# Retention and mixture of experts on one core: a list read as it lies, gate operations a tile sooner, and four smaller edits

## Chip, cores and metric

The kernel runs as one program on one core of a Trainium2 chip. The metric is device time in microseconds (us), lower is better. TensorE does matrix products, VectorE, ScalarE and GpSimd (POOL in the profile) work element by element, and SyncE (SP) issues most of the DMAs.

## The reference

Retention over 8 sequences of 576 positions, 8 heads of 64, then a layer of 8 experts in which every token goes to the one with the highest logit:

```python
scores = q @ k.T / sqrt(64)                       # (8, 8, 576, 576)
D[h, i, j] = gamma[h] ** (i - j) if i >= j else 0 # gamma = 1 - 2 ** (-5 - h)
x = (scores * D) @ v                              # -> (4608, 512), heads side by side
logits = x @ w_gate                               # (4608, 8)
e_idx = argmax(logits);  gate_w = softmax(logits)[e_idx]
eom = sigmoid(x @ w_output_gate)
for e in range(8):                                # w1: 512 x 1024, w2: 1024 x 512
    y = relu(x[e_idx == e] @ w1[e]) @ w2[e]
    out[e_idx == e] = gate_w * eom[:, e] * y
```

## The kernel before

**Tiles.** The 4608 positions are 36 tiles of 128; tile g is `c = g % 9` within a run of 9 tiles, which is two sequences. The loop over g is the first half of the program, the experts are the second. Every engine executes its instructions in the order in which the code issues them (`manual_schedule`): the order is written by hand, and an instruction that waits holds up all that stand behind it on its engine.

**One tile.** A tile's q, k and v come as three thirds of one buffer `pk` (768 KB, five buffers), issued by SP: the first five tiles in `load_first`, later ones in two parts (q and k, then v) in `load`. GpSimd scales q and v by powers of gamma into `qs` (L351) and `vs` (L356). Those factors `gq_sb` are made by ScalarE at the start (`factors`, L126) from two inputs gq and gk. TensorE transposes k (`k_rows`, L363), makes the scores `sc` one tile ahead (L385) into three PSUM banks, multiplies state and scores into one buffer `o_ps` (`out_x`, L416 and L420) and adds to the state (L402). VectorE masks the scores into `S_sb` (L389). ScalarE copies `o_ps` to `xT`, and VectorE transposes it into the rows of x (`x_rows`, L437); after these two `o_ps` is free for the next tile. SP stores the rows to `xs` in DRAM.

The three banks are zeroed before the loop with products of a zero operand (L555).

**Gating.** Every four tiles make a group of 512 tokens, n = 0 to 8. TensorE makes its logits (L448) at the end of one tile's turn, then the work on them is spread over the next three turns: `gate_a` on VectorE (maxima, the one-hot `oh` and its sum, L451 to L476), `ranks` on TensorE (L486 to L493), `gate_b`, `gate_d` and `gate_c` on VectorE, which end in `meta`, a token's number and weight. GpSimd scatters each token's entry to its slot in its expert's list in DRAM (`lst`, L536), one DMA for 128 tokens.

**From lists to experts.** An expert's list is taken in two parts: part 0 is its first 360 entries, part 1 the next 256. For expert 0 part 0 holds only tokens of the first six groups, so that it can be read before the loop ends. `load_idx` (SP) loads lists of 16-word entries, spread over four quarters of the partitions, and `make_idx` (VectorE) turns them into `idx` (token and weight) and `gidx`, with one operation at L307 and four copies at L311:

```python
rest = NS[part] > 32 * nb
...
        if g == 31:
            make_idx(0, 2, 0)
        if g + 1 < NTILE:
            prep_v(g + 1)
        if 30 < g < 33:
            for t in (0, 1) if g == 31 else (2,):
                gather_rows(t)
```

GpSimd gathers x from `xs`: for expert 0 whole rows by `idx` (`gather_rows`, L199), into a `pk` buffer in part 0 and transposed by TensorE; for the others quarter rows by `gidx` (`gather`, L186), transposed by VectorE. Expert 0's three tiles of part 0 have 128, 128 and 104 rows.

**The experts.** Each product is made in fp32r as three of split halves (hi by hi, hi by lo, lo by hi). Weights are cast by `upper` (ScalarE, the hi half, L160) and `lower` (VectorE, the rest). `mm1` (L250) makes a block of hidden rows over 360 or 256 columns, `mm2` (L266) the output of one tile; ScalarE scales it (L271) and GpSimd scatters the rows to the output (L272). `some(n)` issues the next n waiting scatters or gathers on GpSimd.

Of the kernel before, what the change touches and what calls it, by code (L numbers as in the profile page):

```python
# [51 lines left out]
def tile_retention_moe(  # L52
# [137 lines left out]
    def gather_rows(t, dep=None):  # L190

        if t == 0:
            rows = ld.tile([P, 3, 512], F32, name="pk")
# [5 lines left out]
        after(G.indirect_dma_start(out=XG[0, t], out_offset=None, in_=xs[0:n, :],  # L199
                                   in_offset=bass.IndirectOffsetOnAxis(ap=idx[:, 0, t, 0:1], axis=0),  # L200
                                   bounds_check=n - 1, oob_is_err=False), dep)
# [73 lines left out]
    lists1 = []

    def load_idx(e0, e1, part):
        s0, t0, nb = part * NS[0], part * 4 * TA, NB[part]
# [4 lines left out]
        dmas = []
        if e1 - e0 < 4:

            for e in range(e0, e1):
                v = view[e, :, s0:s0 + 32 * nb].rearrange("a (j t) w -> a j (t w)", t=nb).broadcast_to([4, 32, LW * nb])
                dmas.append(SP.dma_start(out=lists[:, e, t0:t0 + nb].rearrange("p t w -> p (t w)"), in_=v))
                if rest:
                    v = view[e, :, s0 + 32 * nb:s0 + 32 * nb + 32].broadcast_to([4, 32, LW])  # L290
                    dmas.append(SP.dma_start(out=lists[:, e, t0 + nb], in_=v))
        for a in range(4):
            if e1 - e0 >= 4:
                v = view[e0:e1, 0, s0:s0 + 32 * nb].rearrange("e (j t) w -> j e (t w)", t=nb)
                dmas.append(SP.dma_start(out=lists[32 * a:32 * a + 32, e0:e1, t0:t0 + nb].rearrange("j e t w -> j e (t w)"),
                                         in_=v))
                if rest:
                    v = view[e0:e1, 0, s0 + 32 * nb:s0 + 32 * nb + 32].rearrange("e j w -> j e w")
                    dmas.append(SP.dma_start(out=lists[32 * a:32 * a + 32, e0:e1, t0 + nb], in_=v))
# [4 lines left out]
    def make_idx(e0, e1, part):
        n, t0 = (TA, 0) if part == 0 else (CT - TA, TA)
        lists = lists0 if (e0, part) == (0, 0) else lists1[0]
        V.tensor_scalar(out=gidx[:, e0:e1, 4 * t0:4 * (t0 + n)], in0=lists[:, e0:e1, 4 * t0:4 * (t0 + n), 0],  # L307
                        scalar1=4.0, scalar2=quad, op0=ALU.mult, op1=ALU.add)
        for a in range(4):
            q = slice(32 * a, 32 * a + 32)  # L310
            V.tensor_copy(idx[q, e0:e1, t0:t0 + n],  # L311
                          lists[q, e0:e1].rearrange("j e (t u) w -> j e t u w", u=4)[:, :, t0:t0 + n, a, 0:2])
# [138 lines left out]
    def gate_a(n):  # L451
# [10 lines left out]
        V.tensor_tensor(out=fst, in0=fst, in1=desc.broadcast_to([P, GT, E]), op=ALU.mult)
# [91 lines left out]
    for b in banks:  # L554
        T.matmul(b.rearrange("p a b -> p (a b)"), lhsT=zw[:, 0:P], rhs=zw, start=True, stop=True)  # L555
# [326 lines left out]
```

## Time and profile before

| | |
|---|---|
| time, median of 3 runs | 605.94 us (604.21 to 612.22) |
| profiled execution, its own time | 606.38 us |
| its span, first to last instruction | 604.6 us |
| mean granted TensorE clock | 0.994 of full |
| busy: TensorE (PE) | 576.1 us, 95% of the span |
| busy: VectorE (DVE), GpSimd (POOL), ScalarE (ACT) | 327.7, 315.6 and 169.7 us |
| scores of tile 1, 32, 33, 34 and 35 begin | at 10.04, 128.63, 131.76, 140.11 and 143.89 us of the span |

The profile is one execution. PE stands for TensorE's products, PEld for its loads of the stationary operand, which lie beside products; SPq is SP's issue of a DMA. In a row of the timeline stand the start in us of the span, the duration, the engine, the line of the code, the operation, what it writes and reads (`out<-in`), its shape and type, how many instructions stand in a row (x), and in brackets the idle time of the engine before it and what ended that. A row of the waits has the engine, what it was to write and on which line, the engine, buffer and line it waited for, the sum of the waits in us, their number and the longest of them. A row of a stretch has its bounds, its length, for each engine the busy time and the number of instructions, the granted clock, the share of the DMA engines and GB/s.

### The profile page before, as it was taken

To read this page: it belongs to the slowest core of one execution; us is meant where nothing else is said; L and a number is where in the kernel's file an instruction comes from. 1 tells how busy PE (TensorE), PEld (TensorE's weight loads), DVE (VectorE), ACT (ScalarE), POOL (GpSimd) and SP (SyncE) were. 2 spreads that over 40 slices of the span, in tenths; PEclk is the share of its full clock that TensorE was granted. 3 is DMA by queue.
4 is the path that set the end of the run, shared out by engine and by line. 5 is a ranking of instruction groups with operands and counts; after the bars stand their busy time and mean duration, and the time that the engine had idled before them with its cause. 6 is when DMAs were issued, how large, how long until landed. Compare 5 with 4: busy or idle time off the path is not lost. (4 is left out here: it accounts for less than half of the span.)

```text
span 604.6 us, 14060 instructions
## 1 busy us (share of the span) xinstructions
PE 576.1 (95%) x5737; PEld 507.2 (84%) x5737; DVE 327.7 (54%) x655; ACT 169.7 (28%) x360; POOL 315.6 (52%) x333
## 2 busy tenths in 40 slices
PE   7999999888798999999999999999999999999995
PEld 4888888777696889779978997998899799889974
DVE  3566777674661869736732961584186249426300
ACT  5434334333341222132212221222222222212210
POOL 4768898867276734363553455446344535540011
PEclk9999999998999999999999999999999999999998
DMA  8999899877646436323621642262155216321001
GB/s 304 297 321 287 275 277 292 250 212 237 175 116 214 123 127 225 93 89 114 200 98 58 192 149 75 81 232 96 48 179 165 82 53 218 118 68 52 1 36 44
DMA packets 53324, 94.78 MB, mean 157 GB/s; under 512 B 9018, under 2 KB 30971, under 8 KB 53258
## 3 DMA queue, kind: packets, MB, share of 16 engines
q1 hardware_dynamic: 43594, 73.03, 38.2%
q0 software_dynamic: 9232, 20.23, 10.3%
q8 instruction: 46, 0.75, 0.5%
q10 hardware_dynamic: 432, 0.59, 0.3%
q14 instruction: 20, 0.16, 0.1%
HBM read 74.33 MB, written 20.15 MB: 156 GB/s over the span
## 5 line engine op out<-in xcount | busy, mean ns | idle before, releaser
L186 POOL DMA_INDIRECT x_q<-xs,gidx x140 | 148.7, 1062 | 113.2 <-ACT hh L254 70.9
L250 PE MATMUL h_ps<-xh,w1h 128*128 128x360 f32 (+1 forms) x512 | 154.6, 302 | 2.6 <-issue 1.3
L250 PE MATMUL h_ps<-xl,w1h 128*128 128x360 f32 (+1 forms) x512 | 154.6, 302 | 0.3 <-issue 0.3
L250 PE MATMUL h_ps<-xh,w1l 128*128 128x360 f32 (+1 forms) x512 | 154.5, 302 | 0.0
L266 PE MATMUL y_ps<-w2h,hh 128*128 128x512 f32 (+1 forms) x320 | 125.2, 391 | 2.4 <-ACT y L271 1.4
L266 PE MATMUL y_ps<-w2h,hl 128*128 128x512 f32 (+1 forms) x320 | 124.9, 390 | 0.5 <-DVE hl L255 0.5
L266 PE MATMUL y_ps<-w2l,hh 128*128 128x512 f32 (+1 forms) x320 | 124.8, 390 | 0.0
L272 POOL DMA_INDIRECT out_dram<-y,idx x40 | 41.1, 1028 | 122.6 <-ACT y L271 111.9
L250 PEld LDWEIGHTS h_ps<-xh,w1h 128*128 128x128 f32 x512 | 96.1, 188 | 3.5 <-issue 1.8
L250 PEld LDWEIGHTS h_ps<-xh,w1l 128*128 128x128 f32 x512 | 97.1, 190 | 0.2 <-issue 0.2
L250 PEld LDWEIGHTS h_ps<-xl,w1h 128*128 128x128 f32 x512 | 96.1, 188 | 1.1 <-issue 0.5
L254 ACT ACTIVATE hh<-h_ps 128x360 fp32r<-128x360 f32 (+1 forms) x128 | 54.5, 429 | 149.5 <-PE h_ps L250 126.6
L255 DVE SCALAR_TENSOR_TENSOR hl<-h_ps,hh 128x360 fp32r<-128x360 f32 (+1 forms) x128 | 58.6, 474 | 69.0 <-ACT hh L254 58.2
L266 PEld LDWEIGHTS y_ps<-w2h,hh 128*128 128x128 f32 (+1 forms) x320 | 58.8, 184 | 16.6 <-ACT y L271 1.8
L266 PEld LDWEIGHTS y_ps<-w2h,hl 128*128 128x128 f32 (+1 forms) x320 | 58.8, 184 | 15.3 <-DVE hl L255 1.3
L266 PEld LDWEIGHTS y_ps<-w2l,hh 128*128 128x128 f32 (+1 forms) x320 | 58.8, 184 | 13.4
L271 ACT ACTIVATE y<-y_ps,idx 128x512 f32<-128x512 f32 (+1 forms) x40 | 27.5, 689 | 129.7 <-issue 75.3
L389 DVE TENSOR_TENSOR S_sb<-sc,cmat_sb 128x512 f32<-128x512 f32 x72 | 46.1, 681 | 32.2 <-PE sc L385 29.6
L223 DVE TENSOR_TENSOR xl<-x_t,xh 128x512 fp32r<-128x512 f32 (+1 forms) x35 | 23.5, 672 | 63.9 <-ACT xh L220 61.9
L351 POOL TENSOR_TENSOR qs<-pk,gq_sb 128x512 f32<-128x512 f32 x36 | 46.2, 1282 | 13.4 <-DMA pk<-in_pack_dram 6.6
L536 POOL DMA_INDIRECT lst<-meta,sli x36 | 36.1, 1004 | 27.1 <-DVE meta L532 15.6
L420 PE MATMUL o_ps<-S_sb,vs 128*64 128x128 f32 x576 | 40.4, 281 | 1.8 <-DVE xq L437 0.7
(126 smaller groups left out, 604.3 us busy)
## 6 DMA issues: line engine op xcount, KB each, us to landing
st<-in_w_dram SPq DMA_DIRECT2D x61, 512.0 KB
pk<-in_pack_dram SPq DMA_DIRECT2D x31, 512.0 KB
pk<-in_pack_dram SPq DMA_DIRECT2D x35, 256.0 KB
xs<-xq SPq DMA_DIRECT2D x40, 128.0 KB
pk<-in_pack_dram SPq DMA_DIRECT2D x3, 768.0 KB
x_q<-xs,gidx POOLq DMA_INDIRECT x140
xs<-w2h SPq DMA_DIRECT2D x16, 128.0 KB
xs<-w2l SPq DMA_DIRECT2D x16, 128.0 KB
```

The costliest lines, as they stand in the source:

```text
L186: after(G.indirect_dma_start(out=XG[e, t][:, u, :], out_offset=None, in_=xs.rearrange("t (a c) -> (t a) c", a=4), in_offset=bass.IndirectO ...
L223: V.tensor_tensor(out=lo, in0=src[:, :, 0:n], in1=hi.bitcast(F32), op=ALU.subtract)
L250: T.matmul(ps, lhsT=a[:, k, :], rhs=b[:, k, :], start=(j == 0), stop=(j == 3 * KB - 1))
L254: done = A.activation(out=hh, in_=ps, func=AF.Relu)
L255: V.scalar_tensor_tensor(out=hl, in0=ps, scalar=0.0, in1=hh.bitcast(F32), op0=ALU.max, op1=ALU.subtract)
L266: i = T.matmul(ps, lhsT=a[:, c0:c0 + n], rhs=b, start=(j == 0), stop=(j == 3 * FB - 1))
L271: A.activation(out=y, in_=ps, func=AF.Copy, scale=idx.bitcast(F32)[0:n, e, t, 1:2])
L272: G.indirect_dma_start(out=out, out_offset=bass.IndirectOffsetOnAxis(ap=idx[0:n, e, t, 0:1], axis=0), in_=y, in_offset=None, bounds_check= ...
L351: G.tensor_tensor(out=qs[g], in0=pk[g][:, 0].rearrange("p (n i) -> p n i", n=NP), in1=gq_sb[:, c % 5], op=ALU.mult)
L389: V.tensor_tensor(out=S_sb[:, r].rearrange("p (a b) i -> p a b i", a=2), in0=sc[r].rearrange("p (a b) i -> p a b i", a=2), in1=m, op=ALU.mult)
L420: last = T.matmul(part(p, r), lhsT=vs[g][:, 2 * p + r, :], rhs=S_sb[:, r, p, :], start=(state is None and p < 2), stop=True, skip_group_ch ...
L536: i = G.indirect_dma_start(out=lst, out_offset=bass.IndirectOffsetOnAxis(ap=sli[:, t, :], axis=0), in_=m[:, t, :], in_offset=None)
```

## The change

Six edits:

1. **Expert 0's list as it lies.** `load_rows` loads a part of expert 0's list by one DMA: in part 0, 120 partitions take three entries each, so a partition's entry t is a row of tile t. The gathers and the scaling of y use these entries (`entry`) directly. `make_idx` for expert 0 goes; expert 0's tiles of part 0 have 120 rows each (`N0`). The list of expert 1 is loaded at g = 32 in place of g = 29, its index step stands behind the loop, and those of the other lists stand together after the first transpose of expert 1. At g = 31 GpSimd gathers one tile in place of two, at g = 32 two in place of one.
2. **Gate operations a tile sooner.** `gate_a` is cut in two. Its first four operations (transpose, maximum, two comparisons) come right behind the logits, so ahead of the next masks; the others are `gate_e` at the old place.
3. **Parts.** Tile 2 is loaded in three parts and tiles 3 and 4 in two; the second half of `cmat` comes after tile 3.
4. **One bank in bfloat16.** The third bank is zeroed by a product of bfloat16 operands.
5. **A first copy.** A memset of `bump` on VectorE and a copy of it on ScalarE stand ahead of `factors`.
6. **Casts.** The first weight cast comes at the end of turn g = 33, and two behind the loop; before, they stood at g = 33, 34 and 35 ahead of the turn's `out_x`.

```diff
@@ gather_rows
             for i in range(TA):
-                XG[0, i] = rows[:, i]
+                XG[0, i] = rows[0:N0, i]
...
-                                   in_offset=bass.IndirectOffsetOnAxis(ap=idx[:, 0, t, 0:1], axis=0),
+                                   in_offset=bass.IndirectOffsetOnAxis(ap=entry(0, t)[:, 0:1], axis=0),
...
-    def where(t):
+    def where(e, t):
         part = 0 if t < TA else 1
-        t0 = t - part * TA
-        return part, P * t0, min(P, NS[part] - P * t0)
+        t0, w = t - part * TA, P if e or part else N0
+        return part, w * t0, min(w, NS[part] - w * t0)
+
+    def entry(e, t):
+        part, _, n = where(e, t)
+        return idx[0:n, e, t] if e else rows0[part][0:n, t - part * TA]
...
+    def load_rows(part):
+        n = where(0, part * TA)[2]
+        v = lst[part * NS[0]:part * NS[0] + NS[part], :].rearrange("(p t) w -> p (t w)", p=n)
+        read_after(SP.dma_start(out=rows0[part][0:n].rearrange("p t w -> p (t w)"), in_=v))
...
@@ load_first
-        for i in range(3):
-            SP.dma_start(out=pk[1][:, i], in_=pack[1, :, i])
-        SP.dma_start(out=pk[2], in_=pack[2])
-        SP.dma_start(out=cmat_sb[:, 1], in_=cmat[:, 1])
+        for g in range(1, 3):
+            for i in range(3):
+                SP.dma_start(out=pk[g][:, i], in_=pack[g, :, i])
         for g in range(3, 5):
-            SP.dma_start(out=pk[g], in_=pack[g])
+            for p in (slice(0, 2), slice(2, 3)):
+                SP.dma_start(out=pk[g][:, p], in_=pack[g, :, p])
+            if g == 3:
+                SP.dma_start(out=cmat_sb[:, 1], in_=cmat[:, 1])
@@ gate_a
         V.tensor_tensor(out=lm, in0=l, in1=bc(mx), op=ALU.subtract)
+        gt["fst"] = fst
+
+    def gate_e(n):
+        fst, lm = gt["fst"], gt["lm"]
...
@@ ahead of the loop
-    for b in banks:
-        T.matmul(b.rearrange("p a b -> p (a b)"), lhsT=zw[:, 0:P], rhs=zw, start=True, stop=True)
+    for i, b in enumerate(banks):
+        z = zw.bitcast(BF16)[:, 0:512] if i == 2 else zw
+        T.matmul(b.rearrange("p a b -> p (a b)"), lhsT=z[:, 0:P], rhs=z, start=True, stop=True)
+
+    V.memset(bump, 0.0)
+    A.activation(out=bump[:, 0:1], in_=bump[:, 1:2], func=AF.Copy)
@@ the loop
-        if g == 31:
-            make_idx(0, 2, 0)
...
-            for t in (0, 1) if g == 31 else (2,):
+            for t in (0,) if g == 31 else (1, 2):
                 gather_rows(t)
...
-        if 32 < g < 35:
-            low.append(upper(*wl.pop(0)))
         if n >= 0 and 0 < late < 3:
-            (gate_a, gate_b)[late - 1](n)
+            (gate_e, gate_b)[late - 1](n)
         if g == 35:
...
-            low.append(upper(*wl.pop(0)))
...
             logits(n, gt["ps"])
+            gate_a(n)
...
         if g == 29:
-            load_idx(0, 2, 0)
+            load_rows(0)
+        if g == 32:
+            load_idx(1, 2, 0)
+        if g == 33:
+            low.append(upper(*wl.pop(0)))
...
+    low += [upper(*wl.pop(0)) for _ in range(2)]
     lower(*low.pop(0))
...
@@ experts
-    load_idx(0, 2, 1)
+    make_idx(1, 2, 0)
+    load_rows(1)
+    load_idx(1, E, 1)
     load_idx(2, E, 0)
-    load_idx(2, E, 1)
...
-    make_idx(0, 2, 1)
     some(2)
...
     transp(1, 0)
+    make_idx(1, E, 1)
     make_idx(2, E, 0)
-    make_idx(2, E, 1)
```

**On VectorE, one tile of the loop with the gate operations, before** (`x_rows` is L437; `w2h` and `xq` are its buffers; the masks are L389, the gate L454 to L475):

```order
L437 STREAM_TRANSPOSE w2h_2310<-o_ps 128x4x4x32
L389 TENSOR_TENSOR S_sb<-sc_132,cmat_sb 128x512
L389 TENSOR_TENSOR S_sb<-sc_133,cmat_sb 128x512
L454 STREAM_TRANSPOSE lg_ps<-lg_ps 128x128
L458 TENSOR_REDUCE mx<-lg_ps 128x4
L459 TENSOR_TENSOR lg_ps<-lg_ps,mx 128x32
L461 TENSOR_TENSOR lm<-lg_ps,mx 128x32
L462 TENSOR_TENSOR lg_ps<-lg_ps,csm_sb 128x32
L464 TENSOR_REDUCE m_2381<-lg_ps 128x4
L470 TENSOR_TENSOR oh<-lg_ps,m_2381 128x32
L475 TENSOR_REDUCE oh<-oh 128x8
L437 STREAM_TRANSPOSE w2h_2310<-o_ps 128x4x4x32
```

The same place with the change, where `x_rows` is L449, the masks are L401 and the gate is L466 to L492:

```order
L449 STREAM_TRANSPOSE w2h_2318<-o_ps 128x4x4x32
L466 STREAM_TRANSPOSE lg_ps<-lg_ps 128x128
L470 TENSOR_REDUCE mx<-lg_ps 128x4
L471 TENSOR_TENSOR lg_ps<-lg_ps,mx 128x32
L473 TENSOR_TENSOR lm<-lg_ps,mx 128x32
L401 TENSOR_TENSOR S_sb<-sc_138,cmat_sb 128x512
L401 TENSOR_TENSOR S_sb<-sc_139,cmat_sb 128x512
L479 TENSOR_TENSOR lg_ps<-lg_ps,csm_sb 128x32
L481 TENSOR_REDUCE m_2389<-lg_ps 128x4
L487 TENSOR_TENSOR oh<-lg_ps,m_2389 128x32
L492 TENSOR_REDUCE oh<-oh 128x8
L449 STREAM_TRANSPOSE w2h_2318<-o_ps 128x4x4x32
```

Four operations have moved ahead of the two masks; four still stand between the masks and the transpose that frees `o_ps`.

**On VectorE, turn 31, before** (L531 and L532 end the group's `meta`, L307 and L311 are the index step):

```order
L531 RECIPROCAL meta_87<-lg_ps 128x4
L532 COPY meta_87<-toks 128x4
L307 TENSOR_SCALAR gidx<-lists_89,csm_sb 128x2x12
L311 COPY idx<-lists_89 32x2x6 x4
L437 STREAM_TRANSPOSE w2l_2484<-o_ps 128x4x4x32
L389 TENSOR_TENSOR S_sb<-sc_132,cmat_sb 128x512
L389 TENSOR_TENSOR S_sb<-sc_133,cmat_sb 128x512
```

With the change:

```order
L548 RECIPROCAL meta_87<-lg_ps 128x4
L549 COPY meta_87<-toks 128x4
L449 STREAM_TRANSPOSE w2l_2489<-o_ps 128x4x4x32
L401 TENSOR_TENSOR S_sb<-sc_138,cmat_sb 128x512
L401 TENSOR_TENSOR S_sb<-sc_139,cmat_sb 128x512
```

The five operations on the lists are gone from between `meta` and the transpose.

**On GpSimd, turns 31 and 32, before** (L199 is the gather of expert 0's rows; after `idx` it needs nothing of VectorE):

```order
L351 TENSOR_TENSOR qs<-pk,gq_sb 128x512
L356 TENSOR_TENSOR vs<-pk,gk_sb 128x512
L199 DMA pk<-xs,idx 128x512 x2
L351 TENSOR_TENSOR qs<-pk,gq_sb 128x512
L356 TENSOR_TENSOR vs<-pk,gk_sb 128x512
L199 DMA pk<-xs,idx 128x512
L351 TENSOR_TENSOR qs<-pk,gq_sb 128x512
L356 TENSOR_TENSOR vs<-pk,gk_sb 128x512
```

With the change:

```order
L363 TENSOR_TENSOR qs<-pk,gq_sb 128x512
L368 TENSOR_TENSOR vs<-pk,gk_sb 128x512
L201 DMA pk<-xs,rows_90 120x512
L363 TENSOR_TENSOR qs<-pk,gq_sb 128x512
L368 TENSOR_TENSOR vs<-pk,gk_sb 128x512
L201 DMA pk<-xs,rows_90 120x512 x2
L363 TENSOR_TENSOR qs<-pk,gq_sb 128x512
L368 TENSOR_TENSOR vs<-pk,gk_sb 128x512
```

The gathers stand in the same places, one and two in place of two and one; their offsets are now the rows that SP's DMA brings (`rows_90`), not VectorE's `idx`.

More of the change, by code (lines that the diff above doesn't have):

```diff
@@ L32 @@
 NW = (384, 256)
+N0 = 120
 CAP = sum(NS)
@@ L97, in tile_retention_moe @@
     meta = [const.tile([P, GT, LW], I32, name=f"meta{i}") for i in range(2)]
-    lists0 = const.tile([P, 2, TA * 4, LW], I32, name="lists0")
+    lists0 = const.tile([P, 1, TA * 4, LW], I32, name="lists0")
+    rows0 = [const.tile([P, n, LW], I32, name=f"rows{i}") for i, n in enumerate((TA, CT - TA))]
     idx = const.tile([P, E, CT, 2], I32, name="idx")
@@ L215, in split_x @@
     def split_x(e, t, src):
-        part, c0, n = where(t)
+        part, c0, n = where(e, t)
         hi, lo = (a[:, :, c0:c0 + n] for a in xt_of(e, part))
@@ L227, in transp_pe @@
     def transp_pe(t, src):
+        n = where(0, t)[2]
         for k in range(KB):
-            T.transpose(src[:, k, :], XG[0, t][:, P * k:P * k + P], ident)
+            T.transpose(src[:, k, 0:n], XG[0, t][:, P * k:P * k + P], ident[0:n, 0:n])
         return split_x(0, t, src)
@@ L258, in mm2 @@
     def mm2(e, t, between={}):
-        part, c0, n = where(t)
+        part, c0, n = where(e, t)
         ps = pools["ps_y"].tile([P, DM], F32, name="y_ps")[0:n]
@@ L280, in load_idx @@
         rest = NS[part] > 32 * nb
-        lists = lists0 if (e0, part) == (0, 0) else lists1[0]
+        early = (e0, part) == (1, 0)
         view = lst[0:E * NT, :].rearrange("(e a s) w -> e a s w", e=E, a=1)
[L283 to L299, printed above, removed]
@@ L300, in load_idx @@
-        for i in dmas:
-            for j in scat:
-                tc.add_manual_dep(i.ins, j.name, SYNC, reason="reads the list after every scatter so far")
+        if early:
+            v = view[1, :, s0:s0 + 32 * nb].rearrange("a (j t) w -> a j (t w)", t=nb).broadcast_to([4, 32, LW * nb])
+            read_after(SP.dma_start(out=lists0[:, 0, t0:t0 + nb].rearrange("p t w -> p (t w)"), in_=v))
+            v = view[1, :, s0 + 32 * nb:s0 + 32 * nb + 32].broadcast_to([4, 32, LW])
+            read_after(SP.dma_start(out=lists0[:, 0, t0 + nb], in_=v))
@@ new lines, in load_idx, with read_after @@
+        for a in () if early else range(4):
+            q = slice(32 * a, 32 * a + 32)
+            v = view[e0:e1, 0, s0:s0 + 32 * nb].rearrange("e (j t) w -> j e (t w)", t=nb)
+            read_after(SP.dma_start(out=lists1[0][q, e0:e1, t0:t0 + nb].rearrange("j e t w -> j e (t w)"), in_=v))
+            if rest:
+                v = view[e0:e1, 0, s0 + 32 * nb:s0 + 32 * nb + 32].rearrange("e j w -> j e w")
+                read_after(SP.dma_start(out=lists1[0][q, e0:e1, t0 + nb], in_=v))
+    def read_after(i):
+        for j in scat:
+            tc.add_manual_dep(i.ins, j.name, SYNC, reason="reads the list after every scatter so far")
@@ L304, in make_idx @@
     def make_idx(e0, e1, part):
         n, t0 = (TA, 0) if part == 0 else (CT - TA, TA)
-        lists = lists0 if (e0, part) == (0, 0) else lists1[0]
-        V.tensor_scalar(out=gidx[:, e0:e1, 4 * t0:4 * (t0 + n)], in0=lists[:, e0:e1, 4 * t0:4 * (t0 + n), 0],
+        lists = lists0 if (e0, part) == (1, 0) else lists1[0][:, e0:e1]
+        V.tensor_scalar(out=gidx[:, e0:e1, 4 * t0:4 * (t0 + n)], in0=lists[:, :, 4 * t0:4 * (t0 + n), 0],
                         scalar1=4.0, scalar2=quad, op0=ALU.mult, op1=ALU.add)
@@ L311, in make_idx @@
             V.tensor_copy(idx[q, e0:e1, t0:t0 + n],
[L312 removed]
+                          lists[q].rearrange("j e (t u) w -> j e t u w", u=4)[:, :, t0:t0 + n, a, 0:2])
     actx = ExitStack()
@@ L459, in gate_a @@
         V.tensor_tensor(out=fst, in0=l, in1=bc(mx), op=ALU.is_equal)
-        lm = sm.tile([P, GT, E], F32, name="lm")
+        lm = gt["lm"] = sm.tile([P, GT, E], F32, name="lm")
         V.tensor_tensor(out=lm, in0=l, in1=bc(mx), op=ALU.subtract)
+        gt["fst"] = fst
+    def gate_e(n):
+        fst, lm = gt["fst"], gt["lm"]
+        bc = lambda a: a.broadcast_to([P, GT, E])
         V.tensor_tensor(out=fst, in0=fst, in1=desc.broadcast_to([P, GT, E]), op=ALU.mult)
@@ L639, in tile_retention_moe @@
     gt["ps"] = ps_1.tile([P, 512], F32, name="lg_ps")
-    mm1(0, 0, 0, {5: lambda: (logits(NG - 1, gt["ps"]), gate_a(NG - 1))})
+    mm1(0, 0, 0, {5: lambda: (logits(NG - 1, gt["ps"]), gate_a(NG - 1), gate_e(NG - 1))})
     mm1(0, 0, 1, {9: lambda: ranks(NG - 1)})
```

4 lines of the change are left out of this document (2 added, 2 removed).

## Prediction

> **What bounds the kernel now.** I read the page's busy shares first, then TensorE's busy time stretch by stretch.
>
> ```profile
> PE 576.1 (95%) x5737; PEld 507.2 (84%) x5737; DVE 327.7 (54%) x655; ACT 169.7 (28%) x360; POOL 315.6 (52%) x333
> core 0: us, PE busy (x) PEld busy (x) DVE busy (x) ACT busy (x) POOL busy (x), PEclk, DMA share, GB/s
> 0.00:15.00 15.00, 11.04 (x160) 6.84 (x162) 4.73 (x11) 8.19 (x24) 6.48 (x10) 1.00 0.89 304
> 100.00:150.00 50.00, 44.67 (x1004) 37.44 (x996) 30.53 (x92) 17.02 (x38) 39.21 (x48) 0.97 0.78 245
> 150.00:200.00 50.00, 43.39 (x296) 37.63 (x297) 26.27 (x66) 16.70 (x31) 29.28 (x33) 1.00 0.55 159
> 300.00:400.00 100.00, 100.00 (x569) 89.48 (x568) 51.12 (x76) 23.81 (x47) 48.90 (x47) 1.00 0.36 117
> ```
>
> TensorE is busy 576.1 of 604.6 us. From 300 to 400 us it has no gap, and the change leaves the experts' products alone there. So only the other 28.5 us can be won, plus time in which TensorE runs at a lower clock, and the edits sit in three of the stretches that hold it: the start, the loop over tiles, and the loop's end at about 130 us. I take them in order, against the profiled execution's 606.38 us (span 604.6 and 1.8 around it); that is 0.44 above the median of the three runs, 605.94, so I carry no correction.
>
> **The start.** The chain to the third tile's scores (sc, L385), from the timeline:
>
> ```profile
> 1.46 5.28 PE L555 MATMUL sc<-xh 128*128 128x512 f32 x6 [1.46 <-DVE xh L552]
> 6.07 1.28 ACT L126 ACT_TABLE_LOAD   x1 [6.07 <-DMA gk_sb<-in_gk_dram]
> 7.37 1.28 ACT L126 ACTIVATE gq_sb<-gq_sb,gk_sb 128x128 f32<-128x128 f32 x4
> 8.72 1.26 POOL L351 TENSOR_TENSOR qs<-pk,gq_sb 128x512 f32<-128x512 f32 x1 [1.32 <-ACT gq_sb L126]
> 10.04 0.90 PE L385 MATMUL sc<-qs,pk 64*64 64x128 f32 x32 [1.89 <-POOL qs L351]
> 12.30 1.27 POOL L351 TENSOR_TENSOR qs<-pk,gq_sb 128x512 f32<-128x512 f32 x1 [2.31 <-DMA pk<-in_pack_dram]
> 13.62 0.90 PE L385 MATMUL sc<-qs,pk 64*64 64x128 f32 x32 [0.61 <-POOL qs L351]
> 10.00:15.00 5.00, 4.35 (x118) 3.81 (x120) 2.42 (x4) 4.27 (x16) 2.70 (x3) 1.00 1.01 384
> ```
>
> *Table load.* ScalarE stands on gk until 6.07, and only then loads its table. The added copy needs nothing but a memset, so the 1.28 us load lies in that wait, and the factors, qs of tile 1 and sc of tile 1 each come 1.28 us earlier: sc at about 8.8. *Tile 2 in parts.* qs of tile 2 needs the first third alone, but waits for the whole 768 KB. The two other thirds, 512 KB (0.524 MB), take 1.4 us at the 384 GB/s of the last row, so qs starts at about 10.9 and sc of tile 2 at 12.2 instead of 13.62: 1.4 us. Both links move by about the same, so neither becomes the new stop. Bounds for the pair: 0 if the parts land no sooner than the whole, 2.3 (all of POOL's wait) if they land at once; I take **1.4**, from the rate, between the two. Four more DMA issues on SP lie before SP's next work, which waits for sc of tile 1.
>
> *One bank zeroed in bfloat16.* Six passes take 5.28 us, so the third bank's two take 1.76. A bfloat16 product over 512 columns isn't in the trace; its price lies between 0 and those 1.76 us, and I put it at half of one pass, 0.44, so that zeroing ends near 5.4. This is off the chain above (qs of tile 1 decides) and counts 0. The two more instructions at the head (memset, copy) stand in idle time of their engines.
>
> [...] Here the same run of 5.28 us was followed by full speed; a shorter one isn't shown.
>
> **The loop over tiles.** Five cycles of four tiles, from scores to scores, in a table by stretch (the sum), and what TensorE waits for between 30 and 147 us:
>
> ```profile
> sum 75.88, PE 72.58 PEld 62.19 DVE 54.63 ACT 27.68 POOL 65.40; mean PE 14.52 PEld 12.44 DVE 10.93 ACT 5.54 POOL 13.08
> PE o_ps L416 <- DVE w2l L437: 2.2, 1, 2.2
> PE o_ps L416 <- DVE xq L437: 1.2, 2, 0.7
> PE o_ps L416 <- DVE w2h L437: 1.1, 2, 0.6
> PE o_ps L420 <- DVE xq L437: 0.7, 1, 0.7
> ```
>
> A cycle lasts 15.18 us, of which TensorE works 14.52. It waits for L437, VectorE's transpose that frees the only o_ps buffer. One such place, all of VectorE and TensorE that bears on it:
>
> ```profile
> 103.26 1.08 PE L448 MATMUL lg_ps<-xT,wg_sb 128*32 128x128 f32 x32
> 104.28 0.90 PE L385 MATMUL sc<-qs,pk 64*64 64x128 f32 x32
> 105.24 1.29 DVE L389 TENSOR_TENSOR S_sb<-sc,cmat_sb 128x512 f32<-128x512 f32 x2 [1.57 <-PE sc L385]
> 106.44 0.32 DVE L454 STREAM_TRANSPOSE lg_ps<-lg_ps 128x128 f32<-128x128 f32 x1
> 107.48 0.20 DVE L462 TENSOR_TENSOR lg_ps<-lg_ps,csm_sb 128x32 f32<-128x32 f32 x1
> 108.31 0.70 DVE L437 STREAM_TRANSPOSE xq<-o_ps 128x512 f32<-128x512 f32 x1
> 108.45 0.17 PE L493 MATMUL lg_ps<-oh,cbf_sb 128*128 128x8 bf16 x1
> 109.16 0.67 PE L416 MATMUL o_ps<-qs,stT 64*64 64x128 f32 x16 [0.55 <-DVE xq L437]
> ```
>
> The gate operations run from 106.44 to 108.31, ahead of L437. The change moves the first four (106.44 to 107.48, 1.04 us) ahead of S_sb, where VectorE idles 1.57 us. They need the logits, done at about 104.3, so they end at 105.35 and push S_sb from 105.24 to 105.35: 0.1 us, and S_sb is used a whole tile later (it is made before the previous tile's products), so that push is covered. Then come the other gate operations, 0.83, and L437 starts at about 107.5 instead of 108.31 and ends at 108.2, while TensorE finishes its ranks at 108.6: the gap of 0.55 goes. The rows by DVE w2h and xq sum to 3.0 over five places; two smaller ones stand under ACT's names. I take **3.2** for the stage. Bounds: 0 (something else holds the tile), and 0.66 a cycle over seven cycles, 4.6.
>
> **The end of the loop.** Here lies the list of expert 0. SP's issues, VectorE, POOL and TensorE in the timeline, and the same time in two stretches:
>
> ```profile
> 127.67 0.65 SPq L288 DMA_DIRECT2D lists<-lst  x1
> 128.26 1.04 POOL L356 TENSOR_TENSOR vs<-pk,gk_sb 128x512 f32<-128x512 f32 x1
> 129.56 0.54 SPq L291 DMA_DIRECT2D lists<-lst  x1
> 131.76 0.90 PE L385 MATMUL sc<-qs,pk 64*64 64x128 f32 x32
> 133.16 0.24 DVE L307 TENSOR_SCALAR gidx<-lists,csm_sb 128x24 int32<-128x24 int32 x1 [1.64 <-DMA lists<-lst]
> 133.31 0.69 DVE L311 COPY idx<-lists 32x12 int32<-32x12 int32 x4
> 134.04 0.72 DVE L437 STREAM_TRANSPOSE w2l<-o_ps 128x512 f32<-128x512 f32 x1
> 134.90 0.67 PE L416 MATMUL o_ps<-qs,stT 64*64 64x128 f32 x16 [2.24 <-DVE w2l L437]
> 134.91 1.07 POOL L199 DMA_INDIRECT pk<-xs,idx  x1 [5.61 <-DMA xs<-w2h]
> 137.32 1.28 POOL L351 TENSOR_TENSOR qs<-pk,gq_sb 128x512 f32<-128x512 f32 x1
> 132.70:135.00 2.30, 0.10 (x4) 0.13 (x8) 1.74 (x7) 0.00 (x0) 0.09 (x1) 1.00 1.07 328
> 136.10:139.50 3.40, 3.40 (x46) 2.90 (x46) 0.72 (x1) 1.43 (x4) 3.19 (x3) 0.50 1.06 395
> ```
>
> VectorE stands 1.64 us for the lists and makes idx until 134.0, with L437 queued behind it, and TensorE loses **2.24**. POOL's row names a DMA, but it too starts when idx is done. In the change nothing on VectorE waits: one DMA replaces four, its rows are the offsets themselves, and L437 can follow at 131.5, ahead of TensorE's need at 132.6. Right behind the gap the clock is 0.50 for 3.4 us in which TensorE is fully busy: half of it, **1.7**, is lost time. I credit both, 3.9.
>
> The wait moves to POOL, whose gather of the rows now stands for the new list with qs and vs queued behind it. Lists issued last at 129.56 to 130.1 served VectorE at 133.16, 3.1 us on; the new DMA goes out at 127.67 to 128.3, so it lands at about 131.4 at the latest. With one gather (1.07 and 0.3 of issue) qs of tile 34 ends near 134.1; TensorE asks for it a tile (14.52 / 4 = 3.6 us) after 131.76, at 135.4. So POOL's wait is covered by 1.3 us. The two other gathers stand a tile later, behind vs. SP issues 0.65 instead of 2.4 us there, and its later loads come sooner. Bounds: 0 if POOL's new wait stops TensorE for as long, 4.2 with the shorter issue.
>
> [...]
>
> **The rest.** Three weight casts on ScalarE come later, two of them behind the last xT copy; where before they stood ahead of it, the products' first operand could come up to one cast sooner, but xl on VectorE is awaited next: 0, bounds -0.7 and +0.5. In the experts' stage one index step moves some 9 us sooner on VectorE and one some 20 us later, the latter ahead of the gathers that need it; their operations are the same kind (0.24 + 0.69 above), TensorE's products keep their 512 columns, and 120 rows replace 128, 128 and 104. 0, bounds -0.5 and +0.7.
>
> **Sum:** 1.4 + 3.2 + 3.9 = 8.5; 606.38 - 8.5 = 597.9, forecast **598.0**.
>
> **Rivals.** *Another engine holds the tile* (17 in 100): POOL works 65.40 of those 75.88 us, 86%, and its small gaps between scatters bring it near full; if it sets the cycle, the gate edit gives nothing: 597.9 + 3.2 = 601.1. Against it: TensorE's waits name L437, and hardly POOL, after the start. *The half clock stays* (12): 597.9 + 1.7 = 599.6. *More goes* (11): every wait that the loop's cycles show goes (4.6), and the start gives 2.3: 595.6, or a little less if the casts bring their 0.7. *Slower* (5): the full clock isn't granted after the shortened zeroing run. Each us at half clock costs 0.5, so from 17 us of it on, that is until about 24 us, it eats the 8.5; granted only at 30 us, it costs some 12 and gives 609. For it, only that the trace has no shorter run; against it, that TensorE is busy again from 6 us on. That an edit doesn't do what it says is settled by the order of instructions, which shows each in its place.
>
> **Chances and range.** The forecast has 55 in 100, within 595.5 and 600.5. 594 to 603.5 takes in the first three rivals and the bounds of the gate edit and of the clock together (597.9 + 3.2 + 1.7 = 602.8), and leaves out the slow case. 2% is 12.1 us, about what a measurement of this kernel can tell from no change: faster than 593.8 has 6 in 100, slower than 618 has 2, between 92.
>
> **What would show it.** Right: qs of tile 1 at about 7.5 and sc of tile 2 near 12.2; no TensorE wait for L437's successor at the gate tiles, cycles near 14.6; no row for the index step in VectorE's loop, PEclk 1.00 throughout 130 to 150. Wrong: POOL waiting on rows past 134, sc waiting for qs there; a 0.50 stretch anywhere; TensorE at half speed after 6 us.

## The result and the profile after

| | before | changed |
|---|---|---|
| median of 17 runs each | 608.86 us | 601.45 us |
| lowest and highest | 604.21, 614.52 | 598.51, 604.62 |
| ratio, with its 95% interval | | 0.988 (0.9855 to 0.9905) |
| profiled execution | 606.38 us | 602.78 us |

The changed kernel is 1.2% faster, 7.3 us of 608.9; forecast were 8.5 us of 606.4, a ratio of 0.986. The absolute forecast, 598.0, stood on three runs of before with a median of 605.94; over 17 runs that median is 608.86. The 601.45 lie outside the narrower range of the prediction, 595.5 to 600.5, and inside the wider one, 594 to 603.5. Before itself had medians of 596.76, 596.67, 609.31 and 598.20 in the four sets below, each on another chip, so only ratios within a set are compared.

The busy line of the page after, and the five cycles of four tiles by stretch, from scores to scores (36.81 to 111.36 us):

```profile
PE 576.6 (96%) x5736; PEld 509.9 (85%) x5736; DVE 327.7 (55%) x651; ACT 170.6 (28%) x361; POOL 315.7 (53%) x333
sum 74.55, PE 72.48 PEld 61.98 DVE 54.59 ACT 28.07 POOL 64.75; mean PE 14.50 PEld 12.40 DVE 10.92 ACT 5.61 POOL 12.95
```

TensorE's busy time is nearly the same (576.1 before). A cycle lasts 14.91 us (74.55 / 5) against 15.18. The start, in the timeline:

```profile
2.15 1.28 ACT L576 ACT_TABLE_LOAD   x1 [2.15 <-issue]
6.16 1.28 ACT L128 ACTIVATE gq_sb<-gq_sb,gk_sb 128x128 f32<-128x128 f32 x4 [2.51 <-DMA gk_sb<-in_gk_dram]
7.57 1.26 POOL L363 TENSOR_TENSOR qs<-pk,gq_sb 128x512 f32<-128x512 f32 x1
8.89 0.90 PE L397 MATMUL sc<-qs,pk 64*64 64x128 f32 x32 [1.11 <-POOL qs L363]
10.82 1.28 POOL L363 TENSOR_TENSOR qs<-pk,gq_sb 128x512 f32<-128x512 f32 x1 [1.98 <-ACT gq_sb L128]
12.15 0.90 PE L397 MATMUL sc<-qs,pk 64*64 64x128 f32 x32 [0.29 <-POOL qs L363]
```

The table loads at 2.15 instead of 6.07, tile 1's scores begin at 8.89 instead of 10.04, tile 2's at 12.15 instead of 13.62. The gate tile that the prediction showed at 103 to 109 us, TensorE and VectorE:

```profile
104.09 1.08 PE L460 MATMUL lg_ps<-xT,wg_sb 128*32 128x128 f32 x32
105.10 0.90 PE L397 MATMUL sc<-qs,pk 64*64 64x128 f32 x32
105.24 0.33 DVE L466 STREAM_TRANSPOSE lg_ps<-lg_ps 128x128 f32<-128x128 f32 x1 [0.75 <-PE lg_ps L460]
106.17 1.28 DVE L401 TENSOR_TENSOR S_sb<-sc,cmat_sb 128x512 f32<-128x512 f32 x2
108.18 0.71 DVE L449 STREAM_TRANSPOSE xq<-o_ps 128x512 f32<-128x512 f32 x1
109.16 0.67 PE L428 MATMUL o_ps<-qs,stT 64*64 64x128 f32 x16
```

The transpose that frees o_ps comes 3.08 us after the scores' start instead of 4.03, and TensorE's next product has no wait in its row, where it had 0.55. What TensorE still waits for between 15 and 145 us, with the sum, the number and the longest:

```profile
PE o_ps L432 <- issue: 1.6, 4, 0.9
PE o_ps L428 <- issue: 1.2, 1, 1.2
PE st_ps L414 <- issue: 1.0, 1, 1.0
PE sc L397 <- issue: 0.9, 2, 0.6
PE o_ps L428 <- DVE xq L449: 0.4, 1, 0.4
PE o_ps L428 <- DVE sli L529: 0.3, 1, 0.3
PE lg_ps L460 <- issue: 0.2, 1, 0.2
PE o_ps L428 <- DVE w2l L449: 0.2, 1, 0.2
```

VectorE's transposes are nearly gone from the list. In their place stand 4.9 us of "issue", waits for nothing that the profile shows, where before had 0.7 in the same stretch. Three of them, 2.46 us between 21.30 and 34.15 us, take back the gain of the start: the scores of tile 8 begin at 36.81 us, against 35.49 before, and those of tile 28 at 111.36, against 111.37. Up to there these two profiles show no gain at all from the start and the gate; the timed parts below do. The end of the loop and what follows, by stretch:

```profile
130.00:150.00 20.00, 17.64 (x376) 14.56 (x376) 14.95 (x39) 11.03 (x21) 14.07 (x17) 1.00 0.98 291
155.00:160.00 5.00, 4.16 (x18) 4.16 (x18) 3.61 (x11) 1.06 (x3) 0.42 (x2) 0.51 0.09 30
160.00:165.00 5.00, 5.00 (x27) 5.00 (x27) 4.02 (x17) 1.10 (x3) 2.80 (x5) 0.81 0.36 108
PE lg_ps L503 <- DVE lm L473: 2.7, 1, 2.7
```

From 130 to 150 us the clock is whole, as forecast, but from 155 to 162 it is half, behind a wait of 2.70 us for the last group's ranks; before waited 2.13 us there and kept its clock. The experts' first product starts 6.4 us sooner than before (147.9 for 154.3), of which 3.3 are lost in the next 23 us.

### The profile page after: what moved, and what is told of

Its sections match the earlier page's. It is cut to its first block, busy times and chain, and to the rows that moved or that the text cites. A ratio compares the mean times of both kernels' runs of the same rounds, so it can differ in the third digit from the quotient of the medians.

```text
span 601.0 us, 14067 instructions
## 1 busy us (share of the span) xinstructions
PE 576.6 (96%) x5736; PEld 509.9 (85%) x5736; DVE 327.7 (55%) x651; ACT 170.6 (28%) x361; POOL 315.7 (53%) x333
## 5 line engine op out<-in xcount | busy, mean ns | idle before, releaser
L258 PE MATMUL h_ps<-xh,w1h 128*128 128x360 f32 (+1 forms) x512 | 156.6, 306 | 3.1 <-issue 1.9
L274 PE MATMUL y_ps<-w2h,hh 128*128 128x512 f32 (+2 forms) x320 | 125.1, 391 | 1.4 <-ACT y L279 1.4
L274 PE MATMUL y_ps<-w2l,hh 128*128 128x512 f32 (+2 forms) x320 | 124.9, 390 | 0.0
L274 PE MATMUL y_ps<-w2h,hl 128*128 128x512 f32 (+2 forms) x320 | 124.7, 390 | 0.0
L280 POOL DMA_INDIRECT out_dram<-y,idx x35 | 35.5, 1015 | 115.8 <-ACT y L279 105.5
L274 PEld LDWEIGHTS y_ps<-w2h,hh 128*128 128x128 f32 (+2 forms) x320 | 58.8, 184 | 15.5 <-ACT y L279 1.8
L274 PEld LDWEIGHTS y_ps<-w2h,hl 128*128 128x128 f32 (+2 forms) x320 | 58.8, 184 | 14.1
L274 PEld LDWEIGHTS y_ps<-w2l,hh 128*128 128x128 f32 (+2 forms) x320 | 58.8, 184 | 13.5
L401 DVE TENSOR_TENSOR S_sb<-sc,cmat_sb 128x512 f32<-128x512 f32 x72 | 46.3, 684 | 21.1 <-PE sc L397 17.4
L279 ACT ACTIVATE y<-y_ps,idx 128x512 f32<-128x512 f32 (+1 forms) x35 | 24.1, 688 | 118.4 <-issue 67.1
L242 DVE STREAM_TRANSPOSE x_t<-x_q 128x512 f32<-128x512 f32 x35 | 24.7, 705 | 31.6 <-DMA x_q<-xs,gidx 31.6
```

What stands on the lines that cost most here:

```text
L242: V.transpose(out=src.rearrange("p k (u j) -> p u k j", u=4), in_=XG[e, t].rearrange("p u (k i) -> p u k i", k=KB))
L258: T.matmul(ps, lhsT=a[:, k, :], rhs=b[:, k, :], start=(j == 0), stop=(j == 3 * KB - 1))
L279: A.activation(out=y, in_=ps, func=AF.Copy, scale=entry(e, t).bitcast(F32)[:, 1:2])
L401: V.tensor_tensor(out=S_sb[:, r].rearrange("p (a b) i -> p a b i", a=2), in0=sc[r].rearrange("p (a b) i -> p a b i", a=2), in1=m, op=ALU.mult)
```

## The experiments

Every kernel was timed in five rounds beside the kernel before on its chip.

**Each part alone.** One chip, before at 596.76 us.

*The start* (edits 3, 4 and 5):

```diff
-            SP.dma_start(out=pk[g], in_=pack[g])
+            for p in (slice(0, 2), slice(2, 3)):
+                SP.dma_start(out=pk[g][:, p], in_=pack[g, :, p])
...
+    V.memset(bump, 0.0)
+    A.activation(out=bump[:, 0:1], in_=bump[:, 1:2], func=AF.Copy)
```

> The kernel before with edits 3, 4 and 5 alone (first copy, tiles 2 to 4 in parts, one bank in bfloat16). Theory A (the prediction's sum): scores of tile 2 begin at 12.2 instead of 13.62 us and the 1.4 us stay with it to the end, ratio 0.9976. Theory B (TensorE's code arrives no sooner, and the transfers of the first 50 us are full): scores of tile 2 begin at 12.2 as well, but by tile 8 (35.49 before) TensorE has stood for code in gaps that the profile calls issue, near 21, 27 and 33 us as in the changed kernel, and the scores of tile 8 begin between 35.3 and 37; ratio 1.000 to 1.002.

Measured: 0.9978 (0.9957 to 0.9998), 1.3 us: theory A by the time. But the profile has theory B's sign. Two waits named issue stand ahead of tile 8 (at 26.75 and 32.95 us; 2.5 us in all between 15 and 145), and its scores begin at 35.97 us, between 35.3 and 37. The other profiles bear this out. In the nine with the new start and the five with the old one the scores of tile 2 begin at 12.06 and 13.80 us in the mean, those of tile 8 at 35.74 and 35.99; the waits named issue up to there sum to 1.5 and 0.3 us. So of 1.74 us gained at tile 2 only 0.25 are left at tile 8, and by what path the time still gains 1.3 us, in an interval that begins at 0.1, is not shown. The first products of TensorE tell a second thing, in the last row the scores of tile 8:

```profile
6.38 1.56 PE L387 MATMUL sc<-qs,pk 64*64 64x128 f32 x32 [0.72 <-POOL qs L353]
8.91 1.52 PE L387 MATMUL sc<-qs,pk 64*64 64x128 f32 x32
10.36 1.09 PE L422 MATMUL o_ps<-S_sb,vs 128*64 128x128 f32 x16
35.97 0.90 PE L387 MATMUL sc<-qs,pk 64*64 64x128 f32 x32
```

The first two scores take 1.5 us instead of 0.90, and the products from 10.36 us on take what they take in the changed kernel (1.09 in that row). By these times the full clock came only at about 10.3 us in this execution, what the slower rival spoke of, for some 4 us and not for 17 or more. The scores of tile 2 lost some 0.3 us by it (12.43 for 12.15), no more, since GpSimd was late as well. A half clock so early is not the edit's alone: the list edit by itself, with the old start, has one from 11.50 to 14.91 us.

*The gate* (edit 2):

```diff
+            gate_a(n)
...
-            (gate_a, gate_b)[late - 1](n)
+            (gate_e, gate_b)[late - 1](n)
```

> The kernel before with edit 2 alone (four gate operations ahead of the masks). Theory A (the prediction's sum): the five waits for DVE w2h and xq go, cycles of four tiles come down from 15.18 to 14.6 us, 3.2 us in all, ratio 0.9947. Theory B (another engine or the transfers hold the tile): the waits change their name and the cycles stay above 15.0, gain under 1 us, ratio 0.998 to 1.000.

Measured: 0.9943 (0.9918 to 0.9969), 3.4 us: theory A by the time. All waits of TensorE between 15 and 145 us in its profile:

```profile
PE o_ps L416 <- DVE w2l L437: 5.1, 1, 5.1
PE sc L385 <- issue: 2.7, 2, 1.5
PE o_ps L416 <- issue: 0.8, 1, 0.8
PE st_ps L402 <- issue: 0.6, 1, 0.6
PE o_ps L420 <- issue: 0.4, 1, 0.4
```

The waits for w2h and xq are gone; the first row is the list's wait, which this kernel keeps. The four others are theory B's renamed waits, 4.5 us, and a cycle lasts 15.45 us here (34.94 to 112.17 us, five cycles), as B said above 15.0. One of these waits is followed by 3.41 us at half clock:

```profile
93.14 0.67 PE L385 MATMUL sc<-qs,pk 64*64 64x64 f32 x21 [1.48 <-issue]
94.74:98.15 3.41, 3.41 (x42) 2.96 (x42) 2.06 (x8) 1.11 (x3) 2.60 (x4) 0.50 0.79 228
```

The profiled execution was the slowest of the nine (597.48 us, median 594.29), so it does not refute the gain, but it does not show it either. Over all profiles of this study the sum of "issue" in that stretch is 0.7 to 2.6 us in the five without edit 2 and 3.1 to 5.5 us in the nine with it.

*The list* (edit 1):

```diff
-            make_idx(0, 2, 0)
...
-            load_idx(0, 2, 0)
+            load_rows(0)
+        if g == 32:
+            load_idx(1, 2, 0)
```

> The kernel before with edit 1 alone (expert 0's list as it lies, gathers and index steps moved). Theory A (the prediction's sum): no wait of 2.24 us at 132.7 and no 3.4 us at half clock behind it; from the scores of tile 32 to the first product of the experts 25.68 us before, 21.8 then; 3.9 us in all, ratio 0.9936. Theory B (the drop of the clock only moves to the next place where TensorE idles, the wait for the ranks at about 157): the same 3.9 us are gained up to the first product, and 1.7 to 3.4 are lost behind it, ratio 0.996 to 0.999.

Measured: 0.9973 (0.9953 to 0.9992), 1.6 us: theory B's size; 3.9 us (0.9936) lies outside the interval. In the profile there is no wait at 132 and no half clock behind it, and from tile 32's scores to the experts 19.73 us, where the three kernels of this set with the old list took 22.9, 23.1 and 24.7. Nor is there the later drop of the clock by which B explained its size: behind the loop the clock is whole up to the last stretch. But there is a new wait, which neither theory named:

```profile
PE o_ps L430 <- POOL tick L545: 1.5, 1, 1.5
```

*The casts* (edit 6):

```diff
-        if 32 < g < 35:
-            low.append(upper(*wl.pop(0)))
...
+    low += [upper(*wl.pop(0)) for _ in range(2)]
```

> The kernel before with edit 6 alone (weight casts on ScalarE later). Theory A (the prediction's sum): 0, bounds -0.7 and +0.5 us, ratio 0.999 to 1.001; the wait of 1.70 us at 149.7 stays. Theory B (that wait was for the cast in front of ScalarE's copies): it goes, and with it 1.5 us, ratio 0.9975.

Measured: 0.9998 (0.9971 to 1.0024): theory A. The wait of 1.70 us stands neither in this profile nor in that of the start alone, where the casts lie as before, so it says nothing on its cause. The four parts sum to 1.08%; the whole change brought 1.20% in the first set and 0.81 and 1.03% in the two below, so they add up as far as such differences can tell.

**Parts undone, and what holds GpSimd.** A second chip, before at 596.67 us.

*The changed kernel again:*

> The changed kernel once more, as the measure for the other runs of this call and for what repeats in its profile. Theory A (parts add up: start 0.22%, gate 0.57%, list 0.27%, casts 0): ratio to before 0.989. Theory B (they cover each other's waits or the lost time moves on): 0.992 to 0.995. If the waits named issue at 21.3 and 32.9 us (1.00 and 1.21) belong to the changed kernel, they return here within 0.3 us of those sizes; if they vary from run to run, they are below 0.7 or elsewhere.

Measured: 0.9919 (0.9889 to 0.9949), with both theories in the interval. The waits of 1.00 and 1.21 us at 21.3 and 32.9 did not return in place or size, but the sum of such waits did (5.2 us). The new wait is there, 2.04 us. GpSimd, SP and TensorE in the timeline:

```profile
133.86 0.66 SPq L299 DMA_DIRECT2D lists<-lst  x1
134.56 0.58 SPq L301 DMA_DIRECT2D lists<-lst  x1
137.40 0.10 POOL L552 MEMSET tick<- 128x1 f32 x1
142.30 1.06 POOL L553 DMA_INDIRECT lst<-meta,sli  x1 [4.80 <-PE sc L237]
143.39 1.05 POOL L368 TENSOR_TENSOR vs<-pk,gk_sb 128x512 f32<-128x512 f32 x1
144.49 1.84 PE L432 MATMUL o_ps<-S_sb,vs 128*64 128x128 f32 x16 [2.04 <-POOL tick L552]
145.00:150.00 5.00, 5.00 (x56) 4.07 (x53) 2.67 (x5) 3.43 (x4) 4.43 (x8) 0.69 0.61 131
```

SP reads expert 1's list at 133.86 to 135.1, at turn 32 now. GpSimd's next scatter writes that list and may do so only when the read has landed, which in the semaphores of this trace is at 141.3 to 141.5. So GpSimd stands 4.80 us (the row names TensorE, but the scatter follows the landing: in all six profiles with that load at turn 32 GpSimd stands 4.27 to 5.17 us and starts it 1.3 to 1.7 us after the last packet of the two reads), and behind the scatter stands vs of the last tile, for which TensorE waits 2.04 us and then loses part of its clock (0.69 of full over 5 us). Of the six, five have this wait of TensorE, 1.1 to 2.6 us; only the first profile of the changed kernel, in which TensorE came late itself, has not.

*Without the list edit* (edits 2 to 6 on the kernel before):

> The changed kernel with edit 1 undone, so the start, the gate and the casts alone. Theory A (the list is worth the 3.9 us of the sum): 3.9 us slower than the changed kernel, ratio to before 0.9952 where that has 0.989. Theory B (a drop of the clock happens elsewhere when it does not happen behind the list, so that only the wait itself is gained, and less): 1.6 us slower, ratio to before 0.9915, mean granted clock lower by under 0.002. In the profile the wait for VectorE at 130 us is back with 2 to 5 us and a half-clock window of 3.4 us behind it.

Measured: 0.9954 (0.9929 to 0.9978), so the list edit is worth 0.0035 of 596.67, 2.1 us, nearer to B than to A; the intervals overlap. The mean granted clock is 0.0019 lower than that of the changed kernel (0.9923 and 0.9942), as B said. Start, gate and casts together brought 2.7 us here, where measured apart they sum to 4.8; that lies outside this interval, though the errors of the three parts leave it open. The old wait is back, with half clock behind it:

```profile
131.20 0.67 PE L418 MATMUL o_ps<-qs,stT 64*64 64x128 f32 x16 [3.57 <-DVE w2l L439]
131.00:135.00 4.00, 3.80 (x56) 3.21 (x60) 2.06 (x4) 0.96 (x2) 3.46 (x4) 0.70 0.98 305
```

*The third bank in float32:*

```diff
-    for i, b in enumerate(banks):
-        z = zw.bitcast(BF16)[:, 0:512] if i == 2 else zw
-        T.matmul(b.rearrange("p a b -> p (a b)"), lhsT=z[:, 0:P], rhs=z, start=True, stop=True)
+    for b in banks:
+        T.matmul(b.rearrange("p a b -> p (a b)"), lhsT=zw[:, 0:P], rhs=zw, start=True, stop=True)
```

> The changed kernel with edit 4 undone: the third bank is zeroed in float32 again (six passes, 5.3 us). Theory A (the prediction's sum: zeroing is off the chain): 0, within 0.3 us of the changed kernel. Theory B (five passes end too soon for the clock in a part of the runs, as where tile 0's scores took 1.56 us instead of 0.90 with edits 3 to 5 alone): full clock in every run from 6.4 us on, 0.3 to 1.0 us faster than the changed kernel in the mean.

Measured: 0.9919 (0.989 to 0.9948), the same as the changed kernel: theory A. Its mean granted clock over 12 runs was 0.9953 beside 0.9942 over 6, too near to call.

*The ranks later:*

```diff
-    mm1(0, 0, 0, {5: lambda: (logits(NG - 1, gt["ps"]), gate_a(NG - 1), gate_e(NG - 1))})
-    mm1(0, 0, 1, {9: lambda: ranks(NG - 1)})
+    logits(NG - 1, gt["ps"])
+    gate_a(NG - 1)
+    gate_e(NG - 1)
+    mm1(0, 0, 0)
+    mm1(0, 0, 1)
...
+    mm1(0, 0, 2, {5: lambda: ranks(NG - 1)})
```

> The changed kernel with the last group's logits ahead of the experts' first product instead of after its fifth, and the ranks in the third hidden block (after 5 products) instead of in the second (after 9). Theory A (the wait of 2.70 us for the ranks at 153.1 and the half clock of 6.8 us behind it are lost time): no wait for DVE there, no 0.50 stretch at 155 to 162; 2 to 5 us faster than the changed kernel where that wait shows, and about 1 us on a chip whose profiles do not show it. Theory B (VectorE and ScalarE, which do the gate operations of that group before the first hidden blocks, become late instead): the wait moves to the third block or to a hidden block's bank, gain under 0.5 us.

Measured: 0.9941 (0.9916 to 0.9966), no gain, and inconclusive: on this chip the changed kernel does not wait for the ranks, so there was nothing to win. Here the new wait at L432 was the longest, 2.64 us, with 6.8 us of half clock behind it.

**The list of expert 1.** A third chip, before at 609.31 us. The measure for this set:

> The changed kernel a third time, as the measure for the two other runs of this call. Ratio to before 0.988 to 0.992. Theory A (the list of expert 1, loaded at turn 32, holds up GpSimd's scatters): TensorE waits 1.5 to 2.7 us for GpSimd at L432 near 142 us, with GpSimd idle for 4 to 5 us ahead of a scatter (L553), as in the profiles of the earlier runs with edit 1. Theory B: it doesn't repeat.

Measured: 0.9897 (0.9843 to 0.9951). GpSimd idle for 5.00 us ahead of that scatter, TensorE's wait at L432 1.07 us: the mechanism repeats, the wait below the range named.

*Expert 1's list at turn 29:*

```diff
         if g == 29:
             load_rows(0)
-        if g == 32:
             load_idx(1, 2, 0)
```

> The changed kernel with the two DMAs of expert 1's list issued at turn 29, right behind the rows of expert 0, instead of at turn 32; nothing on VectorE waits for them there. Theory A (a scatter may write the lists only when the read of them has landed, and GpSimd's vs of the last tile stands behind that scatter): no idle time of GpSimd above 2 us ahead of L553 near 137 to 142, no wait of TensorE at L432 there, no half-clock window behind it; 1.5 to 3 us faster than the changed kernel, ratio to before 0.984 to 0.988. Theory B (GpSimd waits there for something else, or two more issues of SP at turn 29 cost as much as they bring): the wait stays or another takes its place, within 0.5 us of the changed kernel.

Measured: 0.9856 (0.981 to 0.9901), median 600.80 beside 602.59. And once more, on a fourth chip (before at 598.20):

> The changed kernel with expert 1's list issued at turn 29, a second time, since the first left its size open (0.9856, interval 0.981 to 0.9901, beside 0.9897 for the changed kernel on the same chip). Theory A (the wait for the list of expert 1 was worth 1.5 to 3 us): ratio to before 0.984 to 0.988, and no idle time of GpSimd above 2 us ahead of L553 near 138. Theory B (its place is taken by other waits): 0.989 to 0.992.

Measured: 0.9859 (0.9815 to 0.9902). GpSimd and TensorE of this run:

```profile
138.33 1.06 POOL L553 DMA_INDIRECT lst<-meta,sli  x1 [0.17 <-issue]
139.42 1.05 POOL L368 TENSOR_TENSOR vs<-pk,gk_sb 128x512 f32<-128x512 f32 x1
143.78 1.09 PE L432 MATMUL o_ps<-S_sb,vs 128*64 128x128 f32 x16
```

The scatter follows after 0.17 us, and vs of the last tile is ready 3.3 us ahead of TensorE, which stood 1.29 us for gathered rows in between. In both profiles the wait of TensorE for GpSimd at L432 is gone, so its cause is shown. That the time falls with it is likely, not shown: twice 0.986 against 0.988, 0.992 and 0.990, with intervals that overlap. This version is the fastest of the study.

*The list edit alone, with expert 1's list at turn 29:*

> The kernel before with edit 1 alone, and in it expert 1's list issued at turn 29 instead of 32. Theory A (the term of 3.9 us was right for the wait at turn 31, and what was missing came from the list of expert 1): 3.9 us faster than before, ratio 0.9935, where edit 1 as it is gave 0.9973. Theory B (the term itself was too large, since a drop of the clock comes elsewhere): ratio 0.996 to 0.998.

Measured: 0.9969 (0.9939 to 0.9998), 1.9 us: theory B's size. The profile shows why A failed here: TensorE waited 2.22 us at 132.7, as if nothing had been changed, though no index step stands there. VectorE and GpSimd:

```profile
131.44 2.74 DVE L542 COPY meta<-toks 128x4 int32<-128x4 int32 x1
134.09 0.70 DVE L447 STREAM_TRANSPOSE w2l<-o_ps 128x512 f32<-128x512 f32 x1
130.72 1.12 POOL L201 DMA_INDIRECT pk<-xs,rows  x1 [1.36 <-DMA lists<-lst]
131.86 1.29 POOL L361 TENSOR_TENSOR qs<-pk,gq_sb 128x512 f32<-128x512 f32 x1
133.09 1.05 POOL L366 TENSOR_TENSOR vs<-pk,gk_sb 128x512 f32<-128x512 f32 x1
```

A copy of four words, 0.14 us at its other places, took 2.74 us and ended with GpSimd's vs, at 134.1. With the new list GpSimd gathers and works at just that moment, where it used to stand idle.

## Why the prediction came out as it did

**The start: right at its tiles and in the time, not in how far it carries.** Forecast 1.4 us; 1.3 alone (0.1 to 2.6). The instants were met: qs of tile 1 at 7.57 (about 7.5), scores at 8.89 (8.8) and 12.15 (12.2); the row of tile 2 names ScalarE's factors where the prediction looked at the load, and in six of the nine profiles it is the load, so both links do end together. But the sum let the 1.4 us pass to the end, and in the profiles TensorE's waits for code, 1.5 us up to tile 8 in the mean against 0.3 with the old start, take most of it back. *The bank in bfloat16* counted 0 and measured 0; zeroing ended at 5.35 (near 5.4). The condition of the slower rival occurred in one profile, too briefly to matter.

**The gate: right in time, and incomplete in the profile.** Forecast 3.2 us; 3.4 alone (1.8 to 4.9). The named waits for L437 went. Cycles came to 14.9, not 14.6, in the profiled execution, since TensorE now waits under another name: 0.27 us a cycle, 1.9 over the prediction's seven cycles. The rival "another engine holds the tile" looked at GpSimd; what came closest to it was TensorE's own code (below).

**The list: the mechanism right, the size not.** This is the step that failed, the 3.9 us. Measured are 1.6 us alone, 2.1 as the difference with and without, and 1.9 with expert 1's list at turn 29. The step said that nothing on VectorE waits any more and that GpSimd's new wait is covered by 1.3 us, and looked only at the gathers. Three things were left out; what each costs in the median was not separated, and with the first of them undone the edit alone still brought 1.9 us. First, the load of expert 1's list moved from turn 29 to 32, and its cost was taken from SP's issue time alone; GpSimd's scatters write what it reads, and the prediction's own rule, that what is queued behind a new wait counts, was applied to the gathers and not to these scatters: 1.1 to 2.6 us in five of six profiles. Second, with GpSimd at work where it was idle, a copy on VectorE took 2.74 us instead of 0.14 and ended with GpSimd's vs, and TensorE waited 2.22 us, in one of nine profiles with edit 1. Third, the 1.7 us for the clock were credited in full. All six profiles with a wait of TensorE at that place (2.2 to 5.1 us) have a half-clock window of 3.4 us behind it, and none of the eight without, so the drop belongs to the wait. But later waits had a drop of their own in four of those eight (behind the new wait, 2.04 and 2.64 us, and behind the ranks, 2.64 and 2.70): the mean granted clock rose by 0.0016 only (0.9928 over 32 runs of before, 0.9944 over 12 with the list alone), which is 1.0 us of 595.

**The rest: right.** The casts came to nothing (0.9998), and from 300 to 500 us TensorE has no gap in either kernel, so the later index steps cost nothing there.

**The sum: near, in part by luck.** The changed kernel gained 7.3 us in the first set, but 4.8 and 6.3 in the two others that timed it. The list was sized at twice what it brought, and the waits for code were in no term; the first set's 7.3 is the largest of the three.

**The profiles taken alone mislead.** Those of before and after differ by 3.6 us, the medians by 7.4. The after profile has 10.2 us at half clock ahead of the last stretch, against 3.4, which is up to 3.4 us, and 4.2 us more of "issue".

## What to carry to other kernels

When a read is moved, look up who writes what it reads next, and what is queued behind that writer: a wait can return on an engine that the edit does not touch. A wait taken from one engine uncovers the next limit behind it, so credit it once and look for its successor in a profile of that edit alone. Follow a gain to the end of its stage: of 1.74 us at tile 2, tile 8 had 0.25 left. A single profile differs from another of the same kernel by more than the effects sought here; several parts, each timed beside its own before, settled what two profiles could not.

## What the runs showed of the hardware

**TensorE waits for its code, 0.2 to 2.5 us a time.** The "issue" waits stand inside groups of equal products. TensorE in the timeline after, and the row of the page (packets, MB, share) for the queue that the profile names instruction:

```profile
20.91 0.40 PE L414 MATMUL st_ps<-vs,kn 128*64 128x64 f32 x6
22.30 0.51 PE L414 MATMUL st_ps<-vs,kn 128*64 128x64 f32 x10 [1.00 <-issue]
q8 instruction: 46, 0.75, 0.5%
```

Six of sixteen products run, 1.00 us passes, then the other ten. The first three such waits, at 21.30, 27.53 and 32.94, have 127 and 126 products between them.

0.75 MB in 46 packets are 16 KB each; an estimate from these rows, if the packets bring TensorE's 5736 products and as many weight loads, is about 125 of each to a packet. Over the 14 profiles 61 of the 77 waits named issue between 15 and 145 us, 43.8 of their 48.6 us, stand at the same numbers of products whatever the kernel (347, 474, 600, 727 and so on, by steps of 126 or 127), and each of these ends 0.9 to 1.6 us after a packet of this queue has landed. From that spacing and these landings it is concluded that TensorE stands there for its code. The 16 others, of 0.15 to 0.6 us, stand elsewhere and are not explained. The sums are larger with edit 2 than without it; that TensorE, less held up, is sooner at the end of a packet fits this, and why a packet came late was not tried.

**VectorE's copies of meta beside GpSimd's vs end with it.** Of the 126 copies of meta in the 14 profiles 112 took 0.14 us and 14 took 0.22 to 2.74. Each of the 14 ended within 0.07 us after GpSimd's vs, and of the 112 none lay beside a product of GpSimd for more than its last 0.05 us. One of the 14, in the run with the ranks later:

```profile
81.54 1.12 DVE L549 COPY meta<-toks 128x4 int32<-128x4 int32 x1
81.55 1.04 POOL L368 TENSOR_TENSOR vs<-pk,gk_sb 128x512 f32<-128x512 f32 x1
```

The copy ends 0.07 us after vs. What in the hardware makes it so is not shown, nor whether GpSimd's products are ever held up by a copy.

**Some waits of TensorE were followed by a half clock, and others as long were not.** Waits of TensorE of 2.04, 2.22, 2.24, 2.64 and 2.70 us had one or two windows of 3.41 us at half clock behind them, and so had one of 1.48 us (the gate alone). Waits of 2.13 and 2.2 us for the ranks, in the profile of before and with expert 1's list at turn 29, had none. So these runs give no length that decides.

**Sets differ by 12 us.** Before had medians of 596.7 to 598.2 us in three sets and of 608.9 and 609.3 us in the two others. In the latter all five profiles show TensorE waiting 2.1 to 2.7 us for the last group's ranks; in the former none does, beyond 0.2 us. Chip and occasion change together from set to set, so which of the two does it is not shown.
